# An attention block with a gated MLP on one core: first MLP weights loaded earlier, couples of half blocks moved, the last unit's shift issued at once, a weight split moved later

## The chip, the cores and the metric

The kernel runs on one core of a Trainium2 chip. Times are device microseconds of one execution; the time before is the median of three executions. A profile of one further execution says what each engine did: TensorE (PE, with its weight loads as PEld), VectorE (DVE), ScalarE (ACT), GpSimd (POOL), and SyncE (SP), whose queue issues all DMAs in this kernel.

## The reference

```python
x = A_x                                   # 1 x 2048 x 512, float32
xn = layernorm(x)
q, k, v = split(xn @ wqkv)                # 32 heads of 16
p = softmax(einsum("bhqd,bhkd->bhqk", q, k) * 16 ** -0.5)
s = einsum("bhqk,bhkd->bhqd", p, v).merge_heads() @ wo
h = maximum(xn @ w1 + b1, 0) ** 2         # 512 -> 1792
g = silu(h @ w2 + b2)                     # 1792 -> 512
return x + s * g
```

## The kernel before

Precision: most products are made of two parts, a high one and a remainder, in three terms (high by high, high by low, low by high). `split` makes the two parts of a weight or of an activation, mostly on POOL, partly with ACT for the high part.

**Lanes.** Heads have 16 dimensions, and with their two parts and the shift they fill 64 rows. So most matmuls use one half of PE's rows, 64, and two of them, one on the upper half (lane 0) and one on the lower (lane 1), run side by side when they stand next to each other in PE's order. PE's order is written out by hand; in the main loop so are those of ACT, DVE, POOL and SP. Before the main loop SP's order is left to the scheduler.

**Three stages.** First comes a stage of layernorm, transposes and the first projections. It ends with the loads of the first K tiles, `ka` (8 DMAs by `load_k`), and Q tiles, `qm`. Then the *lead*: eight groups (`lead_group`), each with four projection tiles (48 matmuls a lane) and, woven in at the positions in `LEAD_AT`, max products. `event(b)` is called at every quarter of a group, b from 0 to 31, and does what is due there: loads, stores of the normalised x (`xn_d`, 1 MB each), and splits of the weight `wr_t`, which comes in two parts through one raw tile `wv`. Last comes the main loop.

**Units and steps.** A unit is four heads by 512 queries; there are 32 units, numbered u = 0 to 31, and 16 steps in each, one for each 128 keys: 512 steps, st = 16 u + key block. A step has four score matmuls (`exp_mm`, L1230), four exps on ACT (L1236), and two steps later four matmuls with V (`pv_step`, L379), which the trace counts as eight. After a unit's last V products ACT copies the result out (`evac`, L389), at the beginning of the half that starts with st % 16 == 2.

**Max products and shifts.** A softmax needs its row maxima before the scores: 64 max products a unit (`max_mm`, L306 on PE, L314 on DVE), 2048 in all, made ahead of the unit that needs them. When a unit's are done, `max_end` puts it in the list `late`, and `shift` reduces the maxima on DVE (L339 to L347), writes them to memory (`keep`, L350) and reads them back as rows of the Q tile `qe` (`back`, `shift_rows`, L370). The unit's first score matmul needs these rows. `later(n, fn)` runs `fn` n steps on; `True` puts it ahead of the others.

**Dense work.** The MLP (`mlp_tasks`, in eight chunks c of 256 rows) and the product with wo (`wo_part`) are woven into the steps as tasks. In chunk 0 a task takes one step (`slot`); later most come as *blocks* of four steps (`long_slots`), in two *halves* of two steps. A half has 12 dense matmul slots on one lane, 8 score matmuls, and on the other lane room for max products: 8 in a plain half, 7 in a *couple's*, where both steps' V products come behind each other. `seven` decides which, two halves at a time. After a block's second half `post` has ACT take the result out of PSUM (ReLU for the MLP's first product, L555). The rows of the weights w1 are read raw into three tiles `ex` (L451), split by POOL into `w1s`, and the first chunk of normalised x is read back as `xc` (L493); the first dense matmuls, in step 4, need both. Once no max products are left, `wide` halves give both lanes dense matmuls: 6 slots and 4 score slots a lane. `oc` holds pieces of the attention's result, read back (L701, L711) after `evac_store` has written them (L426).

Of the kernel before, what the change touches and what calls it, by code (L numbers as in the profile page):

```python
# [8 lines left out]
F32 = mybir.dt.float32  # L9
# [7 lines left out]
P = 128  # L17
S = 2048
D = 512
# [3 lines left out]
KO = D // P  # L23
# [3 lines left out]
NU = NQ * 4  # L27
# [8 lines left out]
EPS = 1e-5  # L36
LEAD_AT = (
    (3, 8, 12, 17, 22, 26, 31, 36, 40, 45, 48),
    (1, 5, 10, 14, 19, 24, 28, 33, 38, 42, 47),
)  # L40


# [1 line left out]
def kernel(  # L44
# [11 lines left out]
    nc = tc.nc  # L56
# [42 lines left out]
    with ExitStack() as ph:  # L99
# [7 lines left out]
        rot = {}  # L107
        turn = {"ka": 0, "qm": 0, "qe": 0}

        def ring(name):  # L110
            t = rot[name][turn[name] % len(rot[name])]
            turn[name] += 1
            return t
# [9 lines left out]
        def fill_ring(name, n, value, rows=(32, 96)):  # L123
            for r in rows:
                nc.gpsimd.memset(rot[name][n][r : r + 32, :].bitcast(F32), value)
# [27 lines left out]
        def load_v(qd):  # L153
            n = NT * 4 * VW
            if "tiles" not in vs:
                vs["tiles"] = [pools["v"].tile([P, n + 16], F32, name=f"v{i}") for i in range(2)]
                for v in vs["tiles"]:
                    nc.gpsimd.memset(v[:, n:], 0.0)
            v = vs["tiles"][qd % 2]
            nc.sync.dma_start(  # L160
                v[:, :n].rearrange("p (t f) -> p t f", t=NT),
                v_d[:, :, 4 * qd * VW : (4 * qd + 4) * VW],
            )
            vs[qd] = v
# [17 lines left out]
        late = []  # L182
        last_use = [None]
        waiting = []
        now = [0]

        def later(n, fn, first=False):
            waiting.insert(0 if first else len(waiting), (now[0] + n, fn))
# [131 lines left out]
        def max_end():  # L320
            while steps[0] < sum(done_m) // 4:
                u, s = divmod(steps[0], 16)
                if s == 15 and min(done_m) < 32 * (u + 1):
                    return
                if s == 11 and min(done_m) < 32 * u + 16:
                    return
                steps[0] += 1
                if s in (3, 11) and u + 1 < NU:
                    load_q_pair(u + 1, "qm", s // 11, qms.setdefault(u + 1, []))
                if s == 15:  # L330
                    late.append((now[0] + 2, u))

        def shift_due(slack=0):
            if late and late[0][0] + slack <= now[0]:
# [2 lines left out]
        def shift(u):  # L337
            sh = sp.tile([P, 3, 16], F32R, name="sh")
            nc.vector.tensor_reduce(sh[:, 0].bitcast(F32), mxs[u], axis=AX.X, op=ALU.max)  # L339
            nc.vector.tensor_reduce(sh[:, 1], mxs[u], axis=AX.X, op=ALU.max, negate=True)  # L340
            with nc.allow_low_precision(reason="the low part of a sum of two, exact in float32"):
                nc.vector.tensor_reduce(
                    sh[:, 2], sh[:, :2].bitcast(F32).rearrange("p i c -> p c i"),
                    axis=AX.X, op=ALU.add, negate=True,
                )
            sq = sp.tile([P, 32], F32, name="sq")
            nc.vector.transpose(sq, sh[:, 1:].rearrange("p i c -> p (i c)").bitcast(F32))  # L347

            def keep():
                nc.sync.dma_start(sh_d[u].rearrange("r (b q) -> b r q", q=32), sq)  # L350

            def back():
                for p in range(2):
                    for i in range(2):
                        shift_rows(u, p, i)

            if in_loop:
                later(1, keep, True)
                later(max(2, 16 * u - 9 - now[0]), back, True)
            else:  # L360
                keep()
                if u < 2:
                    back()
                else:
                    waiting.append((16 * u - 9, back))

        in_loop = []
# [53 lines left out]
        def evac_store(u, ev):  # L421
            qd, qc = divmod(u, 4)
            cs = slice(qc * 512, (qc + 1) * 512)
            for j in range(4):
# [3 lines left out]
                    ev["hl"][32 * j : 32 * j + DH].bitcast(F32),  # L428
                )

        def mlp_tasks(mp):
            wp = mp.enter_context(tc.tile_pool(name="w2p", bufs=1))
            hp = mp.enter_context(tc.tile_pool(name="hp", bufs=1))
            up = right(wstk, "up", 1)
            ex = mp.enter_context(tc.tile_pool(name="ex", bufs=1))
            rot["ex"] = [ex.tile([P, D], F32, name=f"ex{i}") for i in range(3)]
            turn["ex"] = 0
            m1 = ExitStack()
            rp = mp.enter_context(tc.tile_pool(name="rp", bufs=1))
            rs = [rp.tile([P, 2, CW], F32, name=f"r{i}") for i in range(2)]  # L440
# [2 lines left out]
            w2t = wp.tile([P, 2, FO, D], F32R, name="w2t")  # L443
            rot["w1s"] = [wr.tile([P, 2, 2, P], F32R, name=f"w1s{i}") for i in range(8)]
            turn["w1s"] = 0

            raws = []

            def load_w1(fo):
                raw = ring("ex").rearrange("p (a b) -> p a b", b=P)  # L450
                nc.sync.dma_start(  # L451
                    raw, w1[:, fo * P : (fo + 1) * P].rearrange("(ko p) f -> p ko f", p=P)
                )
                raws.append(raw)


            def split_w1(fo):
                raw, ws = raws.pop(0), [ring("w1s") for _ in range(2)]
# [105 lines left out]
            def second(c, tt):  # L564
# [44 lines left out]
                if not tt:  # L609
                    yield from halves(mms[36:], (6,), post, 1)  # L610

            load_w1(0)
            load_xc(0)
            for fo in (1, 2):
                load_w1(fo)
            state["w"] = []
            split_w1(0)
            later(1, lambda: [split_w1(1), load_w1(3)])
# [28 lines left out]
        def right(stk, name, bufs):  # L647
            return stk.enter_context(tc.tile_pool(name=name, bufs=bufs, side="right"))
# [18 lines left out]
        def wo_pools():  # L667
            wos["f"] = right(wstk, "fp", 8)
            wos["oc"] = right(wstk, "ocp", 1)
            tail["p"] = right(wstk, "tailp", 1)  # L670
            free_pt.extend(
                tail["p"].tile([P, 512], F32, name=f"pt{NPT + i}") for i in range(3)
            )
# [263 lines left out]
        st = right(ln, "wq_st", 1)  # L937
        lx = ExitStack()
        xp = lx.enter_context(tc.tile_pool(name="xp", bufs=2))
        pools = {}  # L940

        wr_t = cp.tile([P, 2, KO, 6 * P], F32R, name="wr_t")
        wa_t = wqa.tile([P, 2, KO, 2 * P + D], F32R, name="wa_t")
# [5 lines left out]
        def split_w(dst, kos, cols, raw):  # L949
            nc.scalar.activation(dst[:, 0, kos, cols], raw, AF.Copy)  # L950
            nc.gpsimd.tensor_tensor(
                dst[:, 1, kos, cols], raw, dst[:, 0, kos, cols].bitcast(F32), op=ALU.subtract
            )
# [190 lines left out]
        for i in range(NT + 3):  # L1144
# [26 lines left out]
            if i == 11:  # L1171
                raw_r = [load_w("wv", 3 * P, ((P, 3 * P),))]
# [15 lines left out]
        kp2 = ph.enter_context(tc.tile_pool(name="kp2", bufs=1))  # L1188
        make_ring("ka", kp2, (2, 3), S)
        make_ring("qe", kp2, range(4), 512)  # L1190
        for ko in range(KO):
            split_w(wr_t, ko, slice(0, 3 * P), raw_r[0][:, ko])
        qms[0] = []
        for p in range(2):
            for n in range(4):
# [44 lines left out]
        def event(b):  # L1240
            nonlocal after_v, raw_r
            now[0] = b - 100
            max_end()
            shift_due()
            if b in (2, 3):
                fill_ring("ka", b, 1.0)
            if b == 1:
                raw_r = [load_w("wv", 3 * P, ((D + P, 3 * P),))]
            if b == 5:
                for ko in range(KO):  # L1250
                    split_w(wr_t, ko, slice(3 * P, 6 * P), raw_r[0][:, ko])
                ln.close()
                pools["v"] = ph.enter_context(tc.tile_pool(name="vp", bufs=1))
            if b in (4, 5, 8, 9):
                load_q_pair(b // 8, "qe", b % 2, qes.setdefault(b // 8, []))
            if after_v is None and lead[1] == NT and not any(
                kind == "v" or m % 4 == 0 for kind, m, _ in rest
            ) and b % 4 == 0:
                after_v = b
            if after_v is not None:  # L1260
                k = b - after_v
                if k == 0:
                    s1.close()
                    ep = ph.enter_context(tc.tile_pool(name="ep", bufs=1))
                    free_pt.extend(ep.tile([P, 512], F32, name=f"pt{i}") for i in range(NPT))
                    pools["n"] = ph.enter_context(tc.tile_pool(name="np", bufs=1))
                if k == 4:
                    load_v(0)
                if 1 <= k < 9:
                    load_k(1, k - 1)  # L1270
            if b % 2 and b < 16:
                c, i = divmod(b // 2, 2)
                nc.sync.dma_start(
                    xn_d[i, :, :, c * 512 : (c + 1) * 512], xTs[c][:, i].bitcast(F32)
                )
# [67 lines left out]
        def dense():  # L1343
            mp = ExitStack()
            yield from mlp_tasks(mp)
            mp.close()
            wo_pools()
            wo_ask(0)
            wo_ask(1)
            later(8, wo_small)  # L1350
            yield from wo_part()
# [40 lines left out]
        def seven(st):  # L1392
            if couple[0]:
                couple[0] = False
                return True
            kept = 0 if late and st % 4 == 2 else max(0, 450 - st) // 16 * 2
            couple[0] = ahead_m(sum(done_m) + 14 - kept, st + 4)
            return couple[0]

# [169 lines left out]
```

## Time and profile before

| | |
|---|---|
| time, median of 3 | 1630.71 us (1629.46 to 1632.9) |
| profiled execution | 1631.39 us, its span 1629.6 us |
| PE busy | 1612.4 us, 99% of the span |
| DVE busy | 1341.7 us, 82% |
| ACT busy | 1183.7 us, 73% |
| POOL busy | 523.9 us, 32% |
| DMA | 201.44 MB, mean 124 GB/s |
| granted TensorE clock | mean 0.998 |

PE's busy share counts a slot in which one lane works like one in which both do, so it tells little. More can be read from how long the loop takes for a half block of one kind and another, since they repeat: a half ends with the V products of its second step, and the start of those can be followed through the trace. In the lead a group is the unit that repeats.

### The profile page before, as it was taken

How to read it: one execution, taken by the hardware profiler on the slowest of the kernel's cores; microseconds unless marked ns; L12 is line 12 of the kernel's file. 1: busy time of each engine (PE TensorE's matmuls, PEld its weight loads, DVE VectorE, ACT ScalarE, POOL GpSimd, SP SyncE). 2: the span in 40 equal slices, each digit the busy share in tenths (PEclk: the TensorE clock that was granted, in tenths of full speed). 3: DMA queues.
4: the chain of work that ended last, by engine and by line, in shares of the span. 5: the costliest groups of instructions: out<-in, count | busy, mean ns of one | idle time of the engine just before them, and what ended most of it. 6: DMA issues, size and time to landing. Idle time of an engine off the chain costs nothing.

```text
span 1629.6 us, 35392 instructions
## 1 busy us (share of the span) xinstructions
PE 1612.4 (99%) x13639; PEld 963.8 (59%) x13639; DVE 1341.7 (82%) x2326; ACT 1183.7 (73%) x2345; POOL 523.9 (32%) x548
## 2 busy tenths in 40 slices
PE   8999999999999999999999999999999999999998
PEld 6888665556556655664566556645665565554455
DVE  6499888888878888888888888888888888888823
ACT  6311677788777877877777777777877777777775
POOL 6645568223213320331133112312321233213224
PEclk9999999999999999999999999999999999999999
DMA  8785655335242531442343514333432442326343
GB/s 300 208 288 191 207 163 178 111 91 139 60 106 82 150 95 58 115 123 62 88 128 93 131 43 133 101 85 78 144 97 74 106 121 65 95 78 168 109 141 139
DMA packets 150465, 201.44 MB, mean 124 GB/s; under 512 B 50008, under 2 KB 67416, under 8 KB 148760
## 3 DMA queue, kind: packets, MB, share of 16 engines
q1 hardware_dynamic: 150296, 199.17, 41.7%
q8 instruction: 108, 1.77, 0.5%
q14 instruction: 61, 0.50, 0.1%
HBM read 144.84 MB, written 53.99 MB: 122 GB/s over the span
## 4 chain that ended last, share of the span: by engine, by line
PE 92%; DMA 3%; issue 2%; POOL 1%; SPq 1%; ACT 0%; DVE 0%; DVEq 0%; POOLq 0%
PE po L379 29%; PE pd_t L240 17%; PE pm_t L306 16%; PE se L1230 15%; PE pd_t L208 6%; PE se L1030 3%; PE se L991 2%; PE po L1030 2%; PE pd_t L1030 1%; PE pd_t L794 1%; DMA ka<-k_d 1%; PE pm_t L1089 0%; DMA hl<-r_d 0%; DMA xc<-xn_d 0%; DMA on_d<-hl 0%
## 5 line engine op out<-in xcount | busy, mean ns | idle before, releaser
L314 DVE TENSOR_REDUCE mx<-pm_t 128x1 f32<-128x512 f32 x2048 | 1269.0, 684 | 212.0 <-PE pm_t L306 134.1
L1236 ACT ACTIVATE pt<-se 128x512 f32<-128x512 f32 x1745 | 927.3, 615 | 230.3 <-PE se L1230 151.0
L306 PE MATMUL pm_t<-ka,qm 64*128 64x512 f32 x2048 | 793.5, 416 | 1.8 <-DMA ka<-k_d 0.9
L1230 PE MATMUL se<-qe,ka 64*128 64x512 f32 x2016 | 733.2, 412 | 2.0 <-DMA qe<-sh_d 1.6
L379 PE MATMUL po<-pt,v 128*32 128x512 f32 x3554 | 528.3, 603 | 0.0
L306 PEld LDWEIGHTS pm_t<-ka,qm 64*128 64x128 f32 x2048 | 361.3, 184 | 220.3 <-DVE mx L314 200.1
L1230 PEld LDWEIGHTS se<-qe,ka 64*128 64x128 f32 x2016 | 350.9, 184 | 100.5 <-ACT pt L1236 67.9
L240 PEld LDWEIGHTS pd_t<-xc,w1s 64*128 64x128 f32 x2352 | 295.3, 187 | 52.1 <-issue 50.3
L240 PE MATMUL pd_t<-xc,w1s 64*128 64x256 f32 x2352 | 323.2, 286 | 0.0
L240 PE MATMUL pd_t<-w2t,hT 64*128 64x512 f32 x936 | 253.6, 406 | 0.0
L379 PE MATMUL po<-ex,v 128*32 128x512 f32 x542 | 228.8, 603 | 0.0
L1236 ACT ACTIVATE ex<-se 128x512 f32<-128x512 f32 x271 | 163.4, 616 | 45.7 <-PE se L1230 26.2
L240 PEld LDWEIGHTS pd_t<-w2t,hT 64*128 64x128 f32 x936 | 159.2, 184 | 50.0 <-issue 41.9
L379 PEld LDWEIGHTS po<-pt,v 128*32 128x32 f32 x3554 | 87.5, 108 | 152.3 <-issue 138.2
L558 POOL TENSOR_TENSOR r<-r 128x512 f32<-128x512 f32 x49 | 51.0, 1040 | 331.5 <-ACT r L555 331.5
L577 POOL TENSOR_TENSOR u<-u,b_t 128x512 f32<-128x512 f32 x16 | 20.6, 1287 | 361.5 <-ACT u L576 361.5
L208 PE MATMUL pd_t<-w2t,hT 64*128 64x512 f32 x408 | 106.0, 392 | 0.0
L794 PE MATMUL pd_t<-wot,oc 64*128 64x512 f32 x279 | 79.2, 407 | 0.0
L208 PEld LDWEIGHTS pd_t<-w2t,hT 64*128 64x128 f32 x408 | 72.5, 184 | 9.1 <-DVE mx L314 0.7
L417 POOL TENSOR_TENSOR ot<-ot,hl 128x512 f32<-128x512 f32 x31 | 39.9, 1287 | 113.9 <-DMA hl<-r_d 90.5
L84 POOL TENSOR_TENSOR hT<-r,hT 128x512 fp32r<-128x512 f32 x56 | 72.2, 1290 | 4.7
L555 ACT ACTIVATE r<-pd_t,b_t 128x256 f32<-128x256 f32 x98 | 42.1, 495 | 33.0 <-PE pd_t L240 31.7
(137 smaller groups left out, 1195.1 us busy)
## 6 DMA issues: line engine op xcount, KB each, us to landing
w1s<-w_d SPq DMA_DIRECT2D x196, 256.0 KB
xn_d<-xT SPq DMA_DIRECT2D x8, 1024.0 KB
qm<-q_d SPq DMA_DIRECT2D x128, 64.0 KB
qe<-q_d SPq DMA_DIRECT2D x128, 64.0 KB
ka<-k_d SPq DMA_DIRECT2D x32, 256.0 KB
hl<-r_d SPq DMA_DIRECT2D x31, 256.0 KB
k_d<-hl SPq DMA_DIRECT2D x30, 256.0 KB
q_d<-hl SPq DMA_DIRECT2D x15, 512.0 KB
```

The lines of the kernel that those rows point to most:

```text
L84: (lo or nc.gpsimd).tensor_tensor(dst[1], raw, dst[0].bitcast(F32), op=ALU.subtract)
L208: mm = nc.tensor.matmul(out_, lh(r), rh(r), start=first_ and lane == 0, stop=last_ and lane == 1, skip_group_check=True,)
L240: mm = nc.tensor.matmul(out_, lh(r), rh(r), start=first_ and lane == 0, stop=last_ and lane == 1, skip_group_check=True,)
L306: nc.tensor.matmul(ps, qms[u][p][64 * j : 64 * j + 64, qb * P : (qb + 1) * P], kas[qd, p][64 * j : 64 * j + 64, kc * 512 : (kc + 1) * 512] ...
L314: return nc.vector.tensor_reduce(mxs[u][:, c, kc : kc + 1], ps, axis=AX.X, op=ALU.max)
L379: nc.tensor.matmul(po[32 * j : 32 * j + 32, :], vs[qd][:, (4 * kb + j) * VW : (4 * kb + j) * VW + 32], pts[j], start=(kb == 0), stop=(kb = ...
L555: nc.scalar.activation(r[:, i], ps[:, i * CW : (i + 1) * CW], AF.Relu, bias=b1_t[:, fo : fo + 1])
L558: nc.gpsimd.tensor_tensor(r, r, r, op=ALU.mult)
L794: inst = nc.tensor.matmul(ps[lane], oc[r, a, n, ts_], wot[r, b, n], start=m == 0 and (lane == 0 or wide), stop=m == kos and (lane == 1 or ...
L1030: inst = nc.tensor.matmul(out_, lh(r), rh(r), start=first_ and lane == lane0, stop=last_ and lane != lane0, skip_group_check=True,)
L1230: nc.tensor.matmul(se, kas[qd, j // 2][b : b + 64, kb * P : (kb + 1) * P], qes[u][j // 2][b : b + 64, :], start=True, stop=True,)
L1236: return nc.scalar.activation(pts[j], se, AF.Exp, scale=0.25)
```

## The change

It has seven parts.

1. `LEAD_AT` for lane 1: four of eleven positions move by one or two slots (5, 10, 14, 19 become 6, 12, 15, 20). Since the first group takes only positions from 12 on, it has one max product more a lane.
2. The last unit goes into `late` with the present step instead of two steps on, and its `keep` is run at once, its `back` one step on.
3. The pool `ex` is made in the lead, and `load_w1` for the first three tiles is called in the event 16 quarters after V and the first projections are done; in the main loop's first step these loads are gone.
4. The split of `wr_t`'s first part moves from ahead of `load_k` to event 0.
5. The load of its second part, which needs the raw tile back, thereby comes behind that split.
6. `seven` starts no couple at st % 4 == 0 or st % 16 == 2. A couple that starts at st % 4 == 2 has its second half at st % 4 == 0.
7. `kept`, the reserve of max products, is given up whenever a unit stands in `late`.

```diff
 LEAD_AT = (
     (3, 8, 12, 17, 22, 26, 31, 36, 40, 45, 48),
-    (1, 5, 10, 14, 19, 24, 28, 33, 38, 42, 47),
+    (1, 6, 12, 15, 20, 24, 29, 33, 38, 42, 47),
 )
...
                 if s == 15:
-                    late.append((now[0] + 2, u))
+                    late.append((now[0] + (2 if u < NU - 1 else 0), u))
...
-            if in_loop:
+            if u == NU - 1:
+                keep()
+                later(1, back, True)
+            elif in_loop:
                 later(1, keep, True)
                 later(max(2, 16 * u - 9 - now[0]), back, True)
...
-            load_w1(0)
             load_xc(0)
-            for fo in (1, 2):
-                load_w1(fo)
             state["w"] = []
             split_w1(0)
             later(1, lambda: [split_w1(1), load_w1(3)])
...
-        for ko in range(KO):
-            split_w(wr_t, ko, slice(0, 3 * P), raw_r[0][:, ko])
         qms[0] = []
...
+            if b in (0, 5):
+                for ko in range(KO):
+                    split_w(wr_t, ko, slice(b // 5 * 3 * P, (b // 5 + 1) * 3 * P), raw_r[0][:, ko])
             if b == 1:
                 raw_r = [load_w("wv", 3 * P, ((D + P, 3 * P),))]
             if b == 5:
-                for ko in range(KO):
-                    split_w(wr_t, ko, slice(3 * P, 6 * P), raw_r[0][:, ko])
                 ln.close()
...
                     pools["n"] = ph.enter_context(tc.tile_pool(name="np", bufs=1))
+                    ex = exs.enter_context(tc.tile_pool(name="ex", bufs=1))
+                    rot["ex"] = [ex.tile([P, D], F32, name=f"ex{i}") for i in range(3)]
+                    turn["ex"] = 0
                 if k == 4:
                     load_v(0)
+                if k == 16:
+                    for fo in range(3):
+                        load_w1(fo)
...
-            kept = 0 if late and st % 4 == 2 else max(0, 450 - st) // 16 * 2
+            if st % 4 == 0 or st % 16 == 2:
+                return False
+            kept = 0 if late else max(0, 450 - st) // 16 * 2
             couple[0] = ahead_m(sum(done_m) + 14 - kept, st + 4)
             return couple[0]
```

Three places show what moves. The first is SP's order where the lead ends. `k_d` and `q_d` are stores of the lead's last tiles, `ex` the raw w1 tiles, `xc` the first chunk of x, `qm` a Q tile for the max products. Before:

```order
L974 DMA k_d_63<-hl 128x512 x2
L971 DMA q_d_59<-hl 256x1x512
L451 DMA ex_2491<-in_B_w_dram 128x4x128
L493 DMA xc<-xn_d 128x2x256 x4
L451 DMA ex_2492<-in_B_w_dram 128x4x128
L451 DMA ex_2493<-in_B_w_dram 128x4x128
L451 DMA ex_2491<-in_B_w_dram 128x4x128
L136 DMA qm_200<-q_d_57 32x512
```

Now:

```order
L971 DMA k_d_63<-hl 128x512 x2
L968 DMA q_d_59<-hl 256x1x512
L492 DMA xc<-xn_d 128x2x256 x4
L136 DMA qm_200<-q_d_57 32x512
L141 DMA qm_200<-q_d_57 16x512
L136 DMA qm_200<-q_d_57 32x512
L141 DMA qm_200<-q_d_57 16x512
L438 DMA ex_1270<-in_B_w_dram 128x4x128
```

The load of x stands right behind the stores, and the one w1 load that is left there (the fourth tile) behind the Q tile. The three others stand some thirty rows earlier, ahead of a pair of `k_d` stores in the middle of the lead.

The second place is SP's order around the last unit's shift (`sh_d_96`, and its rows `qe_759`, `qe_760`); `g`, `xr` and `oc` are loads for the product with wo, `on_d` is the store of unit 29's result, which the last `oc` load reads. Before:

```order
L701 DMA oc_20029<-on_d_131 128x2x512
L426 DMA on_d_132<-hl 16x2x512 x4
L789 DMA out_dram<-g 128x512
L711 DMA oc_20029<-on_d_132 128x2x512
L726 DMA g<-g_d 128x512
L731 DMA xr<-in_A_x_dram 128x512
L350 DMA sh_d_96<-sq 4x32x32
L370 DMA qe_759<-sh_d_96 2x512 x2
L370 DMA qe_760<-sh_d_96 2x512 x2
L789 DMA out_dram<-g 128x512
```

Now:

```order
L414 DMA hl<-r_d_126 128x1x512
L350 DMA sh_d_96<-sq 4x32x32
L373 DMA qe_759<-sh_d_96 2x512 x2
L373 DMA qe_760<-sh_d_96 2x512 x2
L785 DMA out_dram<-g 128x512
L722 DMA g<-g_d 128x512
L727 DMA xr<-in_A_x_dram 128x512
L697 DMA oc_20032<-on_d_129 128x2x512
L697 DMA oc_20032<-on_d_130 128x2x512
L697 DMA oc_20032<-on_d_131 128x2x512
L429 DMA on_d_132<-hl 16x2x512 x4
```

The shift went from behind the whole group of `oc` loads to ahead of it.

The third place is PE's order at the end of the half of steps 130 and 131 (130 % 16 is 2). Before it is a couple:

```order
L306 MATMUL pm_t<-ka_202,qm_201 128x512
L240 MATMUL pd_t<-xc,w1s_2513 128x256 x2
L306 MATMUL pm_t<-ka_202,qm_201 128x512
L1230 MATMUL se<-qe_758,ka_203 128x512
L379 MATMUL po<-pt_1249,v_1466 32x512
L379 MATMUL po<-pt_1251,v_1466 32x512
L379 MATMUL po<-pt_1253,v_1466 32x512
L379 MATMUL po<-pt_1256,v_1466 32x512
L379 MATMUL po<-pt_1248,v_1466 32x512
L379 MATMUL po<-pt_1244,v_1466 32x512
```

Now it is a plain half:

```order
L240 MATMUL pd_t<-xc,w1s_2522 128x256 x2
L382 MATMUL po<-pt_1260,v_1478 32x512
L382 MATMUL po<-ex_1271,v_1478 32x512
L382 MATMUL po<-ex_1272,v_1478 32x512
L382 MATMUL po<-pt_1259,v_1478 32x512
L240 MATMUL pd_t<-xc,w1s_2522 128x256 x2
L306 MATMUL pm_t<-ka_202,qm_201 128x512
L240 MATMUL pd_t<-xc,w1s_2522 128x256 x2
L306 MATMUL pm_t<-ka_202,qm_201 128x512
L1225 MATMUL se<-qe_757,ka_202 128x512
L1225 MATMUL se<-qe_758,ka_203 128x512 x2
```

The first step's V products moved up between the dense matmuls, and three score matmuls behind them. Counted over the whole of PE's order there are 69 couple halves before and 67 now; plain halves of 12 dense slots stay at 120, and wide halves go from 10 (steps 492 to 511) to 12 (488 to 511).

More of the change, by code (lines that the diff above doesn't have):

```diff
@@ L429, in evac_store, with load_w1 @@
                 )
+        raws = []
+        def load_w1(fo):
+            raw = ring("ex").rearrange("p (a b) -> p a b", b=P)
+            nc.sync.dma_start(
+                raw, w1[:, fo * P : (fo + 1) * P].rearrange("(ko p) f -> p ko f", p=P)
+            )
+            raws.append(raw)
         def mlp_tasks(mp):
@@ L434, in mlp_tasks @@
             up = right(wstk, "up", 1)
-            ex = mp.enter_context(tc.tile_pool(name="ex", bufs=1))
-            rot["ex"] = [ex.tile([P, D], F32, name=f"ex{i}") for i in range(3)]
-            turn["ex"] = 0
             m1 = ExitStack()
@@ L445, in mlp_tasks @@
             turn["w1s"] = 0
[L447 to L454, printed above, removed]
             def split_w1(fo):
@@ L940 @@
         pools = {}
+        exs = ExitStack()
         wr_t = cp.tile([P, 2, KO, 6 * P], F32R, name="wr_t")
@@ L1346, in dense @@
             mp.close()
+            exs.close()
             wo_pools()
```

## The prediction

> **What bounds the kernel now.** I read the page's busy shares and the chain of waits first, then the loop half by half.
>
> ```profile
> span 1629.6 us, 35392 instructions
> PE 1612.4 (99%) x13639; PEld 963.8 (59%) x13639; DVE 1341.7 (82%) x2326; ACT 1183.7 (73%) x2345; POOL 523.9 (32%) x548
> PE 92%; DMA 3%; issue 2%; POOL 1%; SPq 1%; ACT 0%; DVE 0%; DVEq 0%; POOLq 0%
> ```
>
> PE carries 92% of the chain. So a gain must either remove PE slots, pair lanes that ran alone, or close a place where PE waits. The chain leaves PE in few places; the ones that this change touches are these (start, length, what):
>
> ```profile
> 177.04 5.94 DMA xc<-xn_d
> ...
> 1559.60 5.51 DMA on_d<-hl
> ...
> 1567.32 3.53 DMA sh_d<-sq
> 1572.43 1.77 DMA qe<-sh_d
> ```
>
> Next come windows cut where a half's last V products end, one row for each half (length, then each engine's busy time with its count, PE's granted clock, DMA's share, GB/s). First, main-loop halves in the middle: a plain one, the couple of step 130 (evac), its second half of step 132 (behind a ReLU), the plain first half behind a slot section (160), a plain half at an evac place (210), and the couples of steps 244 and 292 behind a ReLU:
>
> ```profile
> core 0: us, PE busy (x) PEld busy (x) DVE busy (x) ACT busy (x) POOL busy (x), PEclk, DMA share, GB/s
> 532.97:538.68 5.71, 5.71 (x58) 3.54 (x58) 4.98 (x9) 4.58 (x10) 2.51 (x3) 1.00 0.66 188
> 538.68:544.40 5.72, 5.72 (x57) 3.80 (x57) 5.29 (x12) 5.51 (x12) 0.62 (x1) 1.00 0.65 198
> 544.40:549.87 5.47, 5.47 (x58) 3.72 (x57) 4.44 (x8) 4.07 (x8) 2.32 (x3) 1.00 0.81 190
> ...
> 623.73:629.54 5.81, 5.81 (x46) 3.31 (x46) 4.77 (x9) 3.94 (x9) 1.91 (x2) 1.00 0.01 3
> ...
> 765.43:771.09 5.66, 5.66 (x46) 2.77 (x46) 4.97 (x9) 4.51 (x10) 0.00 (x0) 1.00 0.25 65
> ...
> 861.50:867.22 5.72, 5.72 (x57) 3.81 (x57) 5.34 (x13) 4.79 (x10) 2.45 (x3) 1.00 0.43 137
> 997.01:1003.09 6.08, 5.76 (x58) 3.85 (x57) 5.35 (x13) 5.15 (x11) 2.81 (x3) 1.00 0.34 107
> ```
>
> PE is "busy" throughout, yet the same couple takes 5.72 where ACT is at 5.51 of 5.72, and 5.47 elsewhere. Second, the end (steps 488, 490, 492, 494, 496, 498):
>
> ```profile
> 1551.60:1557.05 5.45, 5.45 (x44) 2.92 (x36) 0.00 (x0) 4.21 (x9) 5.20 (x5) 1.00 0.38 127
> 1557.05:1562.51 5.46, 5.46 (x45) 2.92 (x37) 2.03 (x6) 4.07 (x8) 0.89 (x2) 1.00 0.89 293
> 1562.51:1566.95 4.44, 4.44 (x44) 2.47 (x36) 0.00 (x0) 3.39 (x8) 0.63 (x1) 1.00 0.45 163
> 1566.95:1571.39 4.44, 4.44 (x44) 2.48 (x36) 1.38 (x2) 4.03 (x10) 0.68 (x1) 1.00 0.71 215
> 1571.39:1579.36 7.97, 6.34 (x44) 3.46 (x36) 0.00 (x0) 4.77 (x10) 1.87 (x2) 0.79 0.32 101
> 1579.36:1583.80 4.44, 4.44 (x44) 2.55 (x36) 2.11 (x4) 3.39 (x8) 0.68 (x1) 1.00 0.03 6
> ```
>
> A wide half takes 4.44; step 496's takes 7.97, with 1.63 of it idle and a mean clock of 0.79.
>
> **The change part by part.**
>
> *The lead.* Two things move: a wait and a slot.
>
> ```profile
> 55.11 0.39 SPq L959 DMA_DIRECT2D wv<-in_A_wqkv_dram  x1
> 55.61 0.44 SPq L136 DMA_DIRECT2D ka<-k_d  x1
> ...
> 65.79 0.47 PE L306 MATMUL pm_t<-ka,qm 64*128 64x512 f32 x1 [0.89 <-DMA ka<-k_d]
> 74.80:88.70 13.90, 13.90 (x124) 12.19 (x122) 13.44 (x23) 3.82 (x8) 5.80 (x6) 1.00 0.72 222
> ...
> 116.60:130.50 13.90, 13.89 (x120) 10.97 (x118) 13.79 (x24) 2.29 (x4) 7.09 (x8) 1.00 0.71 236
> ```
>
> SP's queue issued the second `wv` load, which waited for POOL's split, directly ahead of the K tiles, and lane 1's max product then waited 0.89 us for one. Split and load are now behind the K tiles, but a store of normalised x (1 MB, by the code) now stands ahead of them, and lane 1 needs its tile two slots sooner (12 instead of 14). I take −0.6, within 0 to −0.89. The first group gains one pair slot: a group of 48 + 11 = 59 slots takes 13.90, so 0.24; if DVE were the limit there it would be two reduces, at the 0.61 of the seven in 4.28 us here:
>
> ```profile
> 1547.25 4.28 DVE L314 TENSOR_REDUCE mx<-pm_t 128x1 f32<-128x512 f32 x7 [0.23 <-PE se L1230]
> ```
>
> that is 1.22. The changed positions could also make PE wait for PSUM banks, as DVE is at 13.44 to 13.79 of 13.90 in a full group; PE is not idle in those rows, so I take nothing for it (but see R4). The `wr_t` split and the w1 loads lie on POOL and SP, with 5.80 of 13.90 on POOL. Net: −0.4, from −0.9 to +1.0.
>
> *The first dense step.* Slot step 4 is the second row here, step 5 the third, by the V products' starts:
>
> ```profile
> 174.83 0.56 SPq L451 DMA_DIRECT2D ex<-in_B_w_dram  x1
> 175.44 2.58 SPq L493 DMA_DIRECT2D xc<-xn_d  x4
> 178.06 1.97 SPq L451 DMA_DIRECT2D ex<-in_B_w_dram  x2
> 179.53:184.39 4.86, 4.14 (x31) 2.04 (x29) 3.39 (x6) 2.84 (x6) 2.23 (x4) 1.00 0.91 285
> 184.39:187.26 2.87, 2.87 (x29) 1.84 (x28) 2.04 (x4) 1.78 (x4) 2.57 (x5) 1.00 0.61 168
> ```
>
> Excess 4.86 − 2.87 = 1.99. The chain says that `xc` ended last. `xc` now goes out about 0.6 sooner (one load's issue, 0.56) and no longer behind 256 KB of w1; at the 285 GB/s that this step's queue moved, that is 0.9. So I take −1.5, within 0 and −2.0. The raw w1 tiles come in the lead's middle, tens of microseconds early. Their splits stay on POOL, which has 2.23 of 4.86 there.
>
> *Couples.* Six couples start at an evac half where they cost 5.72 (114, 130, 146, 162, 178, 194, by the windows of each; the quoted 130 stands for them), two behind a ReLU likewise (244, 308), and 292 costs 6.08. A plain half at such a place costs nothing extra (5.66 at step 210), so swapping a couple there with a plain half at a free place saves 5.72 − 5.47 = 0.25 each, and 0.61 for 292: 8 × 0.25 + 0.61 = 2.6. Against it, the first halves behind a slot section (60, 104, 216, 328, 384) now become plain; such a half takes 5.81 against 5.66, so 5 × 0.15 = 0.7. Net −1.9, with ends −2.6 and 0. Work hidden under a plain half at an evac place: ACT's copies, since a plain half's first V products come earlier and hand their bank back earlier.
>
> *Max products done sooner.* One more per lane in the lead, and giving up `kept` when a unit waits, let the max products end before step 488; before, a single one is left there. Steps 488 and 490 become wide: −(5.45 + 5.46 − 2 × 4.44) = −2.0. That is counted off the code's order, so it is my surest term.
>
> *The last unit's rows.* The shift of unit 31 is on DVE at
>
> ```profile
> 1562.29 0.21 DVE L347 STREAM_TRANSPOSE sq<-sh 128x32 f32<-128x32 f32 x1
> ...
> 1557.32 2.76 SPq L426 DMA_DIRECT2D on_d<-hl  x4
> ...
> 1565.25 0.38 SPq L711 DMA_DIRECT2D oc<-on_d  x1
> 1565.68 0.46 SPq L726 DMA_DIRECT2D g<-g_d  x1
> 1566.19 1.09 SPq L731 DMA_DIRECT2D xr<-in_A_x_dram  x1
> 1567.32 0.55 SPq L350 DMA_DIRECT2D sh_d<-sq  x1
> 1570.87 2.02 SPq L370 DMA_DIRECT2D qe<-sh_d  x4
> ```
>
> but its store goes out five microseconds later: SP's queue is held by L711, which waits for the store of `on_d` (5.51 in the chain). Now the shift comes right after the last max product, on DVE about ten microseconds sooner (the max products end near 1552, at the end of the quoted x7 row), with SP's queue free: store at about 1552.3, rows 3.5 us later, landed at about 1560 and needed by step 496, that starts at 1571.39 − 2.0 = 1569.4 on this time scale. Nine microseconds to spare. So step 496 falls to a wide half's 4.44: −(7.97 − 4.44) = −3.5.
>
> What is late next: everything behind the shift on SP. Its store and rows, 0.55 + 3.0 of waiting + 2.02, hold the queue from about 1552.3 to 1557.9 where it stood free for `g`, `xr` and three `oc` loads from 1554.0 on, so these and the `on_d` store move by about 3.9 us, and L711's last piece of `oc` lands at about 1574 (issued at 1565.25 + 3.9, and the four or five microseconds that a load behind a store needed elsewhere in the chain, 5.51 and 5.94 at most). Step 498 needs it at about 1575. That is slack of 0 to 2 us and the thinnest cover in this account.
>
> [...] The row of step 496 shows a clock of 0.79 over 7.97 us, thus about 2 × 0.21 × 7.97 = 3.3 us at half rate, after no more than 1.6 us of idle PE; 1.63 idle + 3.3 / 2 lost = 3.3 of the 3.5 excess. So the trace says that a wait w of that size costs about w + 1.7. [...]
>
> *Sum.* −0.4 − 1.5 − 1.9 − 2.0 − 3.5 = −9.3. The profiled execution took 1631.39 us (span 1629.6 and 1.8 around it), 0.7 above the median of 1630.71. So 1622.1 against its own, and 1621.4 as a median.
>
> **The rivals.**
>
> R1, *the last unit's rows displace `oc`*: L711's piece lands after 1575 and step 498 stalls by w. For it: the slack above, 0 to 2 us. Against it: step 498's row has no idle time, and the slack is above zero at both ends of my estimate. It costs w, and from a w near 1.6 on also the half clock's 1.7: 1621.4 + 0.5 to 3.4, so 1621.9 to 1624.8.
>
> R2, *couples pay anyway*: moved couples have their second half at st % 4 == 0, behind a ReLU, some 17 of them. If those paid 0.25 as first halves do, 4.2 is lost: 1625.6. Against it stands the row of step 132, 5.47 in just that place.
>
> R3, *the first step keeps its excess*: `xc` is bound by its own transfer (5.94 us in the chain with DMA at 0.91), not by w1 in its way. Then −1.5 goes: 1622.9.
>
> R4, *slower*: the lead's new positions put both lanes' max products into one slot (12, 12) and space them less evenly, and PE waits for DVE to give banks back. DVE has only 13.90 − 13.44 = 0.46 idle in one full group and 0.11 in another. If each of seven full groups grows by w, the time ends at 1621.4 + 7 w; it passes 1630.71 at w = 1.3, which is two reduces (1.22) lost in each, and 1634 at w = 1.8. Against it: a full group keeps its 22 reduces, and 22 × 0.61 is 13.4 of 13.9.
>
> **How the numbers follow.** Forecast 0.62; R1 0.13; R2 0.06; R3 0.09; R4 0.10. The likeliest, 1621.4, has its own ends from the lead's −0.9 to +1.0, the first step's 0 to −2.0, the couples' −2.6 to 0, of which I take about half each way: 1619.0 to 1624. The range reaches over R3, R1 and the middle of R2: 1618.5 to 1625.8; outside it are R4 and R1 together with R2. A measurement here tells about 0.2%, that is 3.3 us, from no change. All cases but R4 end more than that below 1630.71, so faster has 0.90; R4 is within it from w = 0.9 to 1.8, 0.04, and slower beyond, 0.06.
>
> **What would show it.** Right: windows of steps 488 to 498 of 4.44 each at a clock of 1.00; no `qe<-sh_d` in the chain at the end; a first dense step of about 3.3; couples of 5.47 everywhere, with 5.8 in five halves behind slot sections; the first group about 0.4 shorter in all. Wrong: a wait named `oc<-on_d` on PE with a clock under 1.00 at step 498 (R1), couples' second halves at 5.7 (R2), `xc<-xn_d` still in the chain at 177 to 184 (R3), lead groups over 14.1 with PE waiting for DVE (R4).

## The result

The changed kernel takes 1623.89 us (median of 6, 1622.95 to 1624.29) against 1630.2 us (median of 6) before: ratio 0.9959, 95% interval 0.9946 to 0.9971, thus 4.7 to 8.8 us faster. Its profiled execution took 1623.24 us, span 1621.4. Span against span it is 8.2 us; of the 1.8 us between that and the medians, 1.2 are that the profiled execution of before was slow for its kernel (1631.39) and 0.65 that the one of after was fast.

The page of after: the chain is PE's to 99% now, and the waits on DMA at the first dense step (`xc`) and at the end (`on_d`, `sh_d`, `qe`) are gone from it.

```profile
span 1621.4 us, 35371 instructions
...
PE 1607.4 (99%) x13639; PEld 963.5 (59%) x13639; DVE 1339.5 (83%) x2327; ACT 1184.9 (73%) x2345; POOL 526.4 (32%) x549
...
PE 99%; DVE 0%; DMA 0%; ACT 0%; issue 0%; SPq 0%; DVEq 0%; ACTq 0%
```

Windows of after, cut like those of before: slot step 4; the plain half of step 60 and the couple of 62; the evac halves of 130 and 162, both plain now; the plain half of 164; and the six halves from 488 to 498.

```profile
178.82:181.98 3.16, 3.16 (x31) 1.89 (x29) 2.94 (x6) 2.52 (x6) 2.99 (x5) 1.00 1.01 313
341.94:347.97 6.03, 6.03 (x58) 3.71 (x58) 4.70 (x9) 3.95 (x9) 4.45 (x4) 1.00 0.00 0
347.97:353.75 5.78, 5.78 (x57) 3.84 (x57) 4.64 (x8) 5.54 (x12) 2.57 (x3) 1.00 0.55 156
536.88:542.55 5.67, 5.67 (x58) 3.50 (x58) 4.71 (x8) 4.59 (x10) 0.51 (x1) 1.00 0.79 221
626.20:631.86 5.66, 5.66 (x46) 2.74 (x46) 4.97 (x9) 4.51 (x10) 0.00 (x0) 1.00 0.21 58
631.86:637.92 6.06, 6.05 (x46) 2.65 (x46) 5.50 (x13) 4.35 (x9) 0.00 (x0) 1.00 0.52 149
1549.42:1553.92 4.50, 4.50 (x38) 2.55 (x38) 0.17 (x1) 4.01 (x8) 4.25 (x5) 1.00 0.05 8
1553.92:1558.36 4.44, 4.44 (x38) 2.52 (x38) 1.38 (x2) 4.03 (x9) 1.86 (x2) 1.00 0.73 208
1558.36:1562.80 4.44, 4.44 (x38) 2.48 (x38) 0.00 (x0) 4.02 (x9) 1.29 (x1) 1.00 0.99 356
1562.80:1567.25 4.45, 4.45 (x38) 2.51 (x38) 1.38 (x2) 4.03 (x9) 1.28 (x1) 1.00 0.50 134
1567.25:1571.69 4.44, 4.44 (x38) 2.52 (x38) 0.00 (x0) 4.02 (x9) 1.29 (x1) 1.00 0.99 344
1571.69:1576.14 4.45, 4.45 (x38) 2.51 (x38) 2.23 (x4) 4.03 (x9) 1.28 (x1) 1.00 0.09 27
```

The end is as forecast: wide halves of 4.44 to 4.50 at full clock, step 496 too. The evac halves are down to 5.66 to 5.70. But 60, 62 and 164 are slower than anything at their places before (5.51, 5.47 and 5.46, couples all). Following the start of V products through both traces, half by half, gives the whole account:

| part of the program | forecast | trace after minus before |
|---|---|---|
| lead, first projection to last | −0.4 | 113.49 to 112.73: −0.8 |
| slot step 4 | −1.5 | 4.86 to 3.16: −1.7 |
| couples and plain halves, steps 60 to 486 | −1.9 | −0.1 |
| steps 488 and 490 | −2.0 | −2.0 |
| step 496 | −3.5 | −3.5 |
| sum | −9.3 | −8.1 |

The couples' term came to nothing. To see why, take as the norm 5.465 for a couple and 5.68 for a plain half (also for two slot steps), and sum what each two steps from 60 to 430 take above it: 5.0 us before, 4.9 after (behind 430 none differs by more than 0.03). The old places are clean, and as much came up at new ones: four couples, 62, 118, 230 and 342, at 5.74 to 5.78 by which of the V products is followed (at least +0.28 each); three plain halves, 164, 180 and 196, at 6.05 to 6.07 (+0.38 each); and plain first halves behind slot sections, 60 (6.04) and 384 (5.97) more than the 5.81 that I had taken. (The half of 384 varies by execution: in four of the runs below that change nothing near it, it takes 5.79 to 5.84.) ACT's and DVE's rows say what stands there. ACT at the couple of 62:

```profile
346.79 1.58 ACT L1231 ACTIVATE pt<-se 128x512 f32<-128x512 f32 x3 [1.48 <-PE se L1225]
348.24 0.64 ACT L581 ACTIVATE r<-u 128x512 f32<-128x512 f32 x1
348.75 3.54 ACT L1231 ACTIVATE pt<-se 128x512 f32<-128x512 f32 x7
352.10 0.92 ACT L554 ACTIVATE r<-pd_t,b_t 128x256 f32<-128x256 f32 x2
```

The Tanh of the MLP's gate (L581, `gate`, due three steps after `post`) is queued ahead of the couple's exps, and all seven behind it are late without a gap. But three of the four places, 62, 230 and 342, were couples before too, with the same Tanh at their front, and took 5.47. ACT before, at 62:

```profile
346.63 2.56 ACT L1236 ACTIVATE pt<-se 128x512 f32<-128x512 f32 x5
349.02 0.68 ACT L582 ACTIVATE r<-u 128x512 f32<-128x512 f32 x1
350.58 3.59 ACT L1236 ACTIVATE pt<-se 128x512 f32<-128x512 f32 x7 [0.88 <-PE pm_t L306]
```

There the half ahead (60) was a couple as well. Its exps end about a microsecond before its V products do (350.1), so the Tanh runs beside these and ACT even waits 0.88 us behind it. Now the half ahead is plain, because part 6 lets couples start at st % 4 == 2 only: its last exps end at 348.4, behind its V products (348.0), and the Tanh comes on top. DVE at the plain half of 164:

```profile
630.23 1.89 DVE L314 TENSOR_REDUCE mx<-pm_t 128x1 f32<-128x512 f32 x3 [0.49 <-PE pm_t L306]
632.03 0.21 DVE L339 TENSOR_REDUCE sh<-mx 128x16 f32<-128x64 f32 x1
632.16 0.21 DVE L340 TENSOR_REDUCE sh<-mx 128x16 fp32r<-128x64 f32 x1
632.40 0.19 DVE L342 TENSOR_REDUCE sh<-sh 128x16 fp32r<-128x32 f32 x1
632.62 0.21 DVE L347 STREAM_TRANSPOSE sq<-sh 128x32 f32<-128x32 f32 x1
632.76 3.04 DVE L314 TENSOR_REDUCE mx<-pm_t 128x1 f32<-128x512 f32 x5
```

The unit's shift now follows a plain half (before, a couple), so the last reduce of that half is still running when the half's own first max products come; the shift, 0.73 us, goes between, and five reduces follow it without a gap.

### The profile page after: what moved, and what is told of

Its sections match the earlier page's. It is cut to its first block, busy times and chain, and to the rows that moved or that the text cites. A ratio compares the mean times of both kernels' runs of the same rounds, so it can differ in the third digit from the quotient of the medians.

```text
span 1621.4 us, 35371 instructions
## 1 busy us (share of the span) xinstructions
PE 1607.4 (99%) x13639; PEld 963.5 (59%) x13639; DVE 1339.5 (83%) x2327; ACT 1184.9 (73%) x2345; POOL 526.4 (32%) x549
## 4 chain that ended last, share of the span: by engine, by line
PE 99%; DVE 0%; DMA 0%; ACT 0%; issue 0%; SPq 0%; DVEq 0%; ACTq 0%
PE po L382 31%; PE pd_t L240 18%; PE pm_t L306 17%; PE se L1225 15%; PE pd_t L208 6%; PE se L988 3%; PE se L1027 3%; PE pd_t L790 2%; PE po L1027 1%; PE pd_t L1027 1%; PE pm_t L1086 0%; PE pm_t L1225 0%; DMA xt<-in_A_x_dram 0%; PE pm_t L824 0%; PE se L872 0%; DVE mx L314 0%
## 5 line engine op out<-in xcount | busy, mean ns | idle before, releaser
L382 PE MATMUL po<-ex,v 128*32 128x512 f32 x556 | 233.9, 603 | 0.0
L1231 ACT ACTIVATE ex<-se 128x512 f32<-128x512 f32 x278 | 166.7, 614 | 49.9 <-PE se L1225 33.3
```

What stands on the lines that cost most here:

```text
L382: nc.tensor.matmul(po[32 * j : 32 * j + 32, :], vs[qd][:, (4 * kb + j) * VW : (4 * kb + j) * VW + 32], pts[j], start=(kb == 0), stop=(kb = ...
L1231: return nc.scalar.activation(pts[j], se, AF.Exp, scale=0.25)
```

## The experiments

Times are medians; "after" is 1623.89. The kernel before, timed again beside these runs, had medians of 1628.9 to 1630.33, so differences of about 1 us between medians of different runs say little by themselves. Where halves are compared, it is by the traces.

**The last unit's shift undone** (part 2):

```diff
-                    late.append((now[0] + (2 if u < NU - 1 else 0), u))
+                    late.append((now[0] + 2, u))
...
-            if u == NU - 1:
-                keep()
-                later(1, back, True)
-            elif in_loop:
+            if in_loop:
```

> The changed kernel without part 2 (the last unit's shift two steps later and its store and rows in the later list again). The prediction's account (part 2 cures step 496): step 496 takes 8.0 us again, the kernel is 3.5 us slower than the changed one. Rival, from the trace after and the order: the max products end before step 488 anyway, so the shift's store stands ahead of unit 29's store on SP even without part 2: step 496 takes 4.44, and the time is that of the changed kernel within 0.3 us in the trace.

1623.28 us, and step 496:

```profile
1568.55:1572.99 4.44, 4.44 (x38) 2.51 (x38) 0.00 (x0) 4.03 (x9) 1.28 (x1) 1.00 0.74 178
```

No half from step 5 on differs from after by more than 0.06. Part 2 is worth nothing in this kernel; the rival holds.

**Part 6 undone:**

```diff
-            if st % 4 == 0 or st % 16 == 2:
-                return False
```

> The changed kernel without the two lines of part 6 (couples may start anywhere). The prediction's account: couples at evac and ReLU places cost 0.25 each again, net 1.9 us slower, nothing else. Rival, from the order: one max product is left at step 488 again, so two wide halves are lost (+2.0), while the couples' sum stays (in the trace after, as much excess came back elsewhere as was removed: 5.0 before, 4.9 after): 2.0 slower, from steps 488 and 490 alone; step 496 stays at 4.44 by part 2.

1626.49 us, 2.6 above after. Steps 488 and 490 are back at couple length, 496 is not back at 8:

```profile
1550.41:1555.87 5.46, 5.46 (x38) 2.92 (x38) 0.00 (x0) 4.06 (x8) 4.81 (x5) 1.00 0.48 156
1555.87:1561.34 5.47, 5.47 (x39) 2.93 (x39) 2.03 (x6) 4.06 (x8) 1.27 (x1) 1.00 0.86 302
1570.22:1574.66 4.44, 4.44 (x38) 2.51 (x38) 0.00 (x0) 4.02 (x9) 1.29 (x1) 1.00 0.60 205
```

Up to step 486 this kernel is 0.9 us slower than after, with two couples more there (a couple takes 0.2 less than a plain half). Couples behind a ReLU cost 5.79 in it (128, 144, 192, 292, 360, 408, 424), evac couples only 5.57 when they are the second of a pair, behind a couple and not behind a plain half (the couples of 66, 82 and 98 show the same before: 5.56). So part 6 is worth 3 us here, two of them by the wide halves, which I had put down to the lead and to part 7.

**Part 6 alone, in the kernel before:** the same two lines added to it.

> The kernel before with the two lines of part 6 alone. If the end of the max products decides steps 488 to 496 (theory since the run without part 2): by the order they end before step 488, two halves become wide (-2.0), the last unit's rows are early enough and step 496 falls from 7.97 to 4.44 (-3.5); 65 couples instead of 67 cost 0.45; so 5 us faster than before, about 1624. The prediction's account: part 6 alone gives -1.9 in the couples and leaves step 496 at 8: 1628.

1625.86 us against 1630.33 (median of 21): ratio 0.9973 (0.9964 to 0.9983). The end is cured by these two lines:

```profile
1551.30:1555.80 4.50, 4.50 (x38) 2.55 (x38) 0.19 (x1) 4.00 (x8) 4.25 (x5) 1.00 0.39 126
1555.80:1560.24 4.44, 4.44 (x38) 2.51 (x38) 1.38 (x2) 4.03 (x9) 1.88 (x2) 1.00 0.96 303
1569.12:1573.56 4.44, 4.44 (x38) 2.49 (x38) 0.00 (x0) 4.03 (x9) 1.29 (x1) 1.00 0.99 323
```

So the max products' end decides it: with one of them left at step 488, two halves stay couples, the shift comes four steps later and falls in behind `oc` on SP. Either part 6 or part 2 takes the wait at 496 away; only part 6 makes the two halves wide. Measured 4.5 faster, expected 5.

This run shows one thing more. It has the old split and the old load of parts 4 and 5, in the same order on SP as before, and yet its lead takes 112.54 us, among the shortest of all: lane 1's max product finds its K tile there without a wait.

```profile
65.33 0.47 PE L306 MATMUL pm_t<-ka,qm 64*128 64x512 f32 x1
```

**The w1 loads undone.** First only the calls went back into the main loop, with the pool `ex` left in the lead:

```diff
-                if k == 16:
-                    for fo in range(3):
-                        load_w1(fo)
...
+            load_w1(0)
             load_xc(0)
+            for fo in (1, 2):
+                load_w1(fo)
```

> The changed kernel with the first three w1 loads back in the main loop, around the load of x. By the trace after, step 4 fell from 4.86 to 3.16 by the loads' place: step 4 takes 4.8 again, 1.7 us slower. Rival: the step gained because the stores ahead of x's load end sooner now, or because the lead is shorter: then step 4 stays under 3.5.

1623.92 us, step 4 within 0.06 of after: a miss. The order shows why: with its tile free in the lead, the first load was put some thirty rows earlier on SP all the same, and only two stood behind `xc`. Then the pool was moved back as well:

> The changed kernel with part 3 undone whole: the loads in the main loop and the pool ex there too, so that the first load stands directly ahead of x's load on SP again (in the run before only two of the three stood behind it, the first one had gone out in the lead). If the load ahead of x is what step 4 waits for: step 4 is 1.0 to 1.7 us longer from the lead's end on (10.0 instead of 8.5 to 8.9 from the lead's end to the end of step 4). If not: 8.5 to 9.1 as in the other runs, and the cause of the old 10.2 stays open.

1625.82 us, and step 4 has its excess again, with `xc` in the chain:

```profile
179.63:184.34 4.71, 4.10 (x30) 2.03 (x28) 3.38 (x6) 2.84 (x6) 2.24 (x4) 1.00 1.03 301
```

```profile
177.63 6.00 DMA xc<-xn_d
184.34 1.07 PE po L382 x8
```

From the end of the lead to that of step 4 it takes 10.1 us (before 10.2, with part 6 alone 9.8); in the eleven kernels whose first load lies in the lead 8.2 to 9.1. So one load of 256 KB directly ahead of `xc` on SP costs 1.1 to 1.6 against the mean of those (8.66), in the three profiles that have it.

**The old positions of the max products** (part 1 undone):

> The changed kernel with the old LEAD_AT. One pair slot less in the first group (-0.23), two max products more in the loop, so 65 couples and 122 plain halves instead of 67 and 120 (+0.45): 0.2 us slower. If the positions made PE wait for DVE in the lead (rival R4 of the prediction, small form), the lead is shorter by more than 0.23 and the time 0.3 or more faster. If the lead's gain of 0.71 came from the positions, the lead gets 0.5 or more longer.

1624.02 us, not to be told from after. As expected, halves 142 and 144 became plain (+0.24 and +0.20). In the lead, the second group goes from 14.0 back to 13.70 and the third from 13.8 to 13.99; without the 0.25 us that PE once waited in the sixth group the lead (112.99) is as long as after's. R4's mechanism is there with 0.3 in one group (in the trace of after, weight loads of max products wait 0.3 us for DVE in it), and 0.2 of it is given back in the next.

**The split of `wr_t` and its load undone** (parts 4 and 5):

> The changed kernel with the split of wr_t's first part ahead of the K loads again (parts 4 and 5 undone). By the prediction the wait of 0.89 us for the K tile comes back: the lead is 0.6 to 0.9 longer. Rival: the gain came from the main stage before the lead, where PE waited for POOL's split (chain rows at 51 to 55 us): then the loss is 1 us or more and stands ahead of the lead.

1624.63 us; the lead takes 114.28 instead of 112.73, from one wait, larger than in the profile of before:

```profile
66.90 0.46 PE L306 MATMUL pm_t<-ka,qm 64*128 64x512 f32 x1 [1.43 <-DMA ka<-k_d]
```

In two of the other kernels with parts 4 and 5 in place a wait of 0.62 to 0.64 us still stands at this product, now put down to POOL's split, which has moved beside it; this is the run without part 2:

```profile
65.39 0.46 PE L306 MATMUL pm_t<-ka,qm 64*128 64x512 f32 x1 [0.62 <-POOL wr_t L945]
```

In the profile of after it is absent. So the wait comes and goes by execution on both sides: with the split and load at the old place it is 0.89 (before), 1.43 (here) and nothing (part 6 alone), with them at the new place 0.62 and 0.64 in two kernels and nothing in nine. The lead takes 112.5 to 114.3 us with the old place and 112.4 to 113.4 with the new. What parts 4 and 5 are worth is not shown, and why the K tile comes late in some executions stays open: the first K tile's load goes out at 55.61 us in the profile of before and at 55.66 in that of after.

**Part 7** has no run of its own: halves start at st % 4 of 0 or 2, and with part 6 ahead of it only st % 4 == 2 reaches the line, where both versions say the same.

**The gate away from the front of a couple:**

```diff
-                    later(3, gate)
+                    later(2 if now[0] % 2 else 3, gate)
```

> The changed kernel with the gate's Tanh (r from u, L581) one step sooner where it fell on an even step, so that it runs in the middle of a half and not at its front. Theory: a couple pays 0.28 for any ACT work queued ahead of its exps; the four couples of steps 62, 118, 230 and 342 (5.75) fall to 5.47 and the first halves behind slot sections that have it (104, 160, 216, 272: 5.80 to 5.84) to 5.68: 1.1 to 1.7 us faster than the changed kernel. Rival: these four couples pay for the ReLU or for POOL: they stay at 5.75 and the time stays.

1622.09 us, 1.8 faster than after by the medians, 1.2 in the trace from step 60 to 486. All four couples fell by 0.29 to 0.30; that of 62:

```profile
347.87:353.34 5.47, 5.47 (x57) 3.74 (x57) 4.53 (x8) 5.14 (x11) 1.49 (x2) 1.00 0.57 172
```

One new +0.30 came up in the couple of 184, and the first halves of 104, 160, 216 and 272 stayed as they were within 0.04, so that part of the expectation missed; what 184 waits for I have not traced.

**Shifts behind couples:**

```diff
-                    shift_due(2 if st < 440 else 0)
+                    shift_due(6 if st < 440 else 0)
```

(at both places in a plain half)

> The changed kernel with the shift held back by six steps in plain halves instead of two, so that the three shifts of steps 163, 179 and 195 run behind the couples of 166, 182 and 198. Theory: a plain half pays 0.38 when DVE's shift (four instructions, 0.73 us) follows a plain half, whose last maximum is still running; behind a couple it costs nothing. Steps 164, 180 and 196 fall from 6.06 to 5.70: 1.1 us faster than the changed kernel. Rival: the cost is the half's own (its place behind an evac half): it stays at 6.06.

1622.84 us, 1.05 faster by the medians, 1.5 in the trace from step 60 to 486. Halves 164, 180 and 196 fell by 0.39, 0.38 and 0.37; that of 164:

```profile
632.85:638.52 5.67, 5.67 (x47) 2.75 (x46) 4.97 (x9) 4.14 (x9) 0.00 (x0) 1.00 0.50 156
```

**Both:**

> The changed kernel with both: the gate in the middle of a half and the shift only behind couples. If the two costs are separate, they add: 2.2 to 2.8 us faster than the changed kernel. If ACT's and DVE's delays are one and the same wait, less than 1.5.

1621.05 us, 2.8 faster by the medians, and 2.7 in the trace from step 60 to 486, where the two alone gave 1.2 and 1.5: they add, ACT's delay and DVE's are two.

**A version that beats both kernels:** gate and shifts as above, the two late shifts only between a plain half's steps, and couples allowed behind slot sections:

```diff
-            if st % 4 == 0 or st % 16 == 2:
+            if st % 4 == 0 and (last_slot[0] != st - 1 or st > 440) or st % 16 == 2:
...
-                    shift_due(2 if st < 440 else 0)
+                    shift_due(6)
```

(`last_slot` holds the last step that was a slot; the second `shift_due` of a plain half is shown, the first one stays as in the run before)

> The changed kernel with the gate in the middle of a half, the shifts behind couples, those of steps 457 and 473 in the middle of the next half, and couples allowed in the first halves behind slot sections. From the halves of the runs so far: gate -1.2, shifts -1.15 (both as measured), the first halves of 60, 104, 160, 216 and 328 fall to 5.42 to 5.52 while as many couples elsewhere become plain, -0.8; the two late shifts -0.2 to -0.4. Together 3.3 us faster than the changed kernel in the trace, about 1620.3. Rival: couples behind slot sections bring the gate's or the ReLU's work ahead of exps elsewhere: then no gain over the kernel with gate and shifts alone (1621.05).

1619.44 us, ratio to before 0.9938 (0.9923 to 0.9953), 4.4 faster than after by the medians and 4.0 in the trace from step 60 to 486, where 3.3 were expected. The halves of 60 and of 458, one of the two late shifts:

```profile
342.11:347.64 5.53, 5.53 (x57) 3.71 (x57) 4.28 (x7) 4.83 (x10) 4.80 (x5) 1.00 0.00 0
1460.89:1466.53 5.64, 5.64 (x43) 2.76 (x43) 5.38 (x13) 4.99 (x10) 0.07 (x1) 1.00 0.67 190
```

Half 458 went from 6.08 to 5.64: DVE's four shift instructions cost nothing between the half's two steps, where the V products leave DVE without new max products, and 0.4 at its front.

**A stall by dose:**

```diff
-                later(1, back, True)
+                later(6, back, True)
```

> The changed kernel with the last unit's rows read back six steps after its store instead of one, so that they stand behind the last load of oc on SP and reach PE late: a dose of a stall of 1 to 2.5 us at step 496. If a stall of this size brings PE's half clock (theory from the row of before): the clock of that half is under 0.85 and the half takes 4.44 plus the idle time plus 1.7. [...]

1623.87 us. The rows came later, but PE waited only 0.33 us for them, not 1 to 2.5:

```profile
1567.43:1572.29 4.86, 4.57 (x38) 2.73 (x38) 0.00 (x0) 4.04 (x9) 1.28 (x1) 1.00 0.49 162
```

```profile
1567.72 0.47 PE L1225 MATMUL se<-qe,ka 64*128 64x512 f32 x1 [0.33 <-DMA qe<-sh_d]
```

It cost 0.42 and the clock stayed at 1.00. The dose was too small to try the prediction's estimate that a wait near 1.6 us costs 1.7 more. Of the halves in the profiles of before and after, only that of step 496 before has the half rate. Cut where its granted clock changes, with a stretch of the same length on each side, that half reads:

```profile
1571.67:1575.08 3.41, 1.78 (x14) 1.11 (x12) 0.00 (x0) 1.53 (x4) 1.59 (x2) 1.00 0.31 87
1575.08:1578.49 3.41, 3.41 (x20) 2.10 (x20) 0.00 (x0) 2.87 (x6) 0.00 (x0) 0.50 0.44 149
1578.49:1581.90 3.41, 3.41 (x34) 2.07 (x27) 0.69 (x1) 1.57 (x5) 0.00 (x0) 1.00 0.00 0
```

The half rate lasts one stretch of 3.41 us in which PE is never idle, behind one in which it was idle for 1.63 us, and then it is gone. The idle time is two waits for `qe`, 1.43 and 0.20 us. Half of 3.41 is the 1.7 of the estimate. A wait of 0.33 us brought no half rate here; from what wait on it comes is not shown, and the estimate still rests on that one half.

## Why the prediction was right, and where not

The time lies in the range, 2.5 us above the point, and the sign and the order of size hold. By its steps:

- *The lead*, −0.4: −0.8 between the two profiles, by the wait that it named (0.89, then none). That moving the split and the load took it away is not shown: with part 6 alone the wait is absent at the old place, and two kernels have it at the new one. That the term came out near is partly luck. The added slot cost 0.1 to 0.2 (the first group without the wait takes 13.2 to 13.4 with the old positions, 13.3 to 13.6 with the new), where 0.24 was said.
- *The first dense step*, −1.5: right in size and cause, by the run with part 3 undone whole. R3 falls.
- *Couples*, −1.9: this is the step that failed. The places left were priced rightly (the evac halves are at 5.66 to 5.70), but I took a couple anywhere else for 5.47 and a plain half in its stead for 5.66. The new order brought 4 × 0.28 by the gate's Tanh and 3 × 0.38 by the shift, and more than I had taken behind slot sections (5 halves, 1.06 in all above 5.66 instead of 0.75); about 0.7 came off at places that I had not counted, 0.24 of it at the couples of 66, 82 and 98. The first two are shown by taking the cause away. I had also named the evac copy and the ReLU as the cause of a dear couple. The rows say that other work of ACT does the same, and that its place decides: at the front of a couple that follows a plain half the Tanh costs 0.28, and behind a couple it cost nothing (62, 230 and 342 before, 5.47); an evac copy costs 0.26 behind a plain half and 0.10 behind a couple (130 and 66 before). The row of step 132, a ReLU that costs nothing behind a couple (5.47), had it.
- *Max products done sooner*, −2.0: right in size, wrong in cause. Neither the lead's positions (still wide from 488 without them) nor `kept` (no effect) bring it, but part 6.
- *The last unit's rows*, −3.5: right in size; part 2 would have been enough, as the run without part 6 shows, but part 6 had already done it.
- R1: the rows went out 2.0 us behind the shift's store, not 3.5 as I had put it, so the queue was held for a shorter time; the last `oc` load followed early enough, and step 498 shows no wait. SP's queue of after:

```profile
1549.61 0.56 SPq L350 DMA_DIRECT2D sh_d<-sq  x1
1551.59 2.03 SPq L373 DMA_DIRECT2D qe<-sh_d  x4
...
1564.95 0.38 SPq L707 DMA_DIRECT2D oc<-on_d  x1
```

- R2: second halves behind a ReLU take 5.47. R4: shown above, 0.3 in one group and given back.

Of the 2.5 us between the point and the median, 1.2 are the terms. The other 1.3 are the median's place beside a profiled execution: I had put it 0.7 below, as it was for before by three runs, and it is 0.65 above the one of after.

## What to carry to other kernels

When work is moved off a crowded place, price the place that it goes to with the same care, from the rows of the engine that is crowded there, and ask what else a fixed delay (three steps after, two steps on) will now put in front of it. Undo a change's parts one at a time, and add one alone to the old kernel: two parts can each be enough for the same gain, and a part can do nothing. A wait that is gone from one pair of profiles is not yet a wait that the change removed: look for it in every other run, those with the old code above all. A small job on a busy engine cost nothing here in the gap where its partner engine does other work (a couple of 5.47 with the Tanh there, a plain half of 5.64 with the shift), and about half of its length at the front of a burst (0.28 of the Tanh's 0.64 us, 0.38 of the shift's 0.73).

## What was not expected of the hardware

The first stage, which no part changes but parts 4 and 5, takes 61.0 to 62.2 us in the profiled executions, up to the lead's first projection, and the wait for a K tile behind it is 0 to 0.64 with the split moved and 0 to 1.43 without: a change below 1 us in the whole time of this kernel can't be told from these. The same half repeats within 0.07 us from run to run, all but that of 384 (5.79 to 5.99).
